# Clustered attention and an MoE layer on one core: PSUM places as one-bank tiles, and a planner that knows tiles, the shared port and the clock

## The chip, the cores and the metric

The kernel runs on one core of a Trainium2 chip. The metric is the device time of one execution in microseconds (us); the time before is the median of three executions. The engines are named as in the profile: PE (TensorE, matmul), PEld (its weight loads), DVE (VectorE), ACT (ScalarE), POOL (GpSimd) and SP (SyncE, which issues every DMA here).

## The reference

Attention in which a query sees only the keys of its own cluster, then a two-layer network with a quadratic activation:

```python
# q, k, v: (4, 8, 768, 64) f32; centroids: (8, 16, 64); w_in: (512, 2048); w_out: (2048, 512)
q_assign = argmax(einsum('bhsd,hcd->bhsc', q_n, c_n)); k_assign = the same of k
mask = q_assign[:, :, :, None] == k_assign[:, :, None, :]
scores = where(mask, q @ k.T / 8, -1e9)
attn = softmax(scores) @ v
x = attn.transpose(0, 2, 1, 3).reshape(3072, 512)
h = x @ w_in
g = where(h >= 1, h, where(h <= -1, 0, (h + 1) ** 2 / 4))
return g @ w_out
```

The two weight matrices come as 64-bit floats.

## The kernel before

The four batches follow each other; in each, four pairs of heads (hp) and three chunks of 256 queries (c). For one batch and pair, `kv_load` loads k, q and v, `kv_scale`, `kq_split` and `v_split` split them into two 16-bit parts, and `assign` finds the clusters: 48 small matmuls into a PSUM place z1 of 128x384, a chain of some ten DVE operations on z1 and the small place pn, and DMA transposes of the result. For each of four blocks of a chunk `at_scores` makes 128x768 scores (4 matmuls), DVE reads them into sS, `at_soft` takes the exponential on ACT (sS), casts it on ACT and subtracts on POOL (hl), and SP transposes hl by DMA into pT. `at_av` multiplies by v (36 matmuls into banka) and gives x. For each chunk u and each of eight slices f of the hidden layer, `ffn1` makes two groups of 12 matmuls from w and x into a place of 128x512, DVE reads that place twice (r), ACT squares and casts, POOL subtracts (g), and `ffn2` adds 12 matmuls of 128x512 to the output place of the chunk. Beside batch 0, `w_load`, `w_bits`, `w_sum` and `w_split` bring the weights into 16-bit parts.

**PSUM before** has eight banks: three tiles of two banks (`bank[0..2]`), `bank_a` for at_av and `bank_h`. The places are slices of them:

```python
halves = [bank[1][:, :512], bank[1][:, 512:]]
row_banks = Ring([bank_h, bank[2][:, :512], bank[2][:, 512:]])
hid = Ring([bank_h] + halves)
spare = Ring([x[:, 384:] for x in halves])
```

`hid` serves ffn1 and ffn_scale in turn, and all small places from step 22 on; up to then (`early()`) those come from `row_banks`, and w_sum's from `spare`. Scores use bank[0], and bank[1] in turn with it while `early()`; ffn2's output uses bank[2]. The framework that sets the semaphores does so tile by tile, and two halves of one tile are one tile to it.

**What sets the order.** The kernel's functions issue nothing: `Recorder.add` (L111) records each operation as a node with its price (`price`, L76) and its region in memory (`touch`, L137), and `issue` (L276) sets the order of all five engines. `forward` (L153) is a list scheduler: it runs the nodes on a model of the engines, the engine that is free first takes the ready node of best priority, and a node with a PSUM bank in use by another engine is put back until the bank is free. `backward` (L231) does this from the end and gives new priorities. After eight rounds (`ROUNDS`) the order with the shortest modelled end is issued by L291, so that nearly every instruction of the profile has the line L291. In the model a DVE operation on SBUF that shares a port with POOL costs 400 ns more (L101), and PE is at half speed for the first 75 us (`COLD`, L216).

Of the kernel before, what the change touches and what calls it, by code (L numbers as in the profile page):

```python
# [33 lines left out]
ROUNDS = 8  # L34

class Recorder:
# [30 lines left out]
    @staticmethod  # L69
    def free(ap):  # L70
        n = 1
        for _, k in list(ap.ap)[1:]:
            n *= k
        return n

    def price(self, eng, op, out, ins, kw):  # L76

        if "dma" in op:
            n = 1
            for k in out.shape:  # L80
                n *= k
            kb = n * mybir.dt.size(out.dtype) / 1024

            return 33, 79.0 if kb == 2 else kb, "transpose" in op
        n = max(self.free(a) for a in [out] + ins[:1])
        ps = any(a.space == PSUM for a in ins)
        cols = sum(isinstance(kw.get(k), bass.AP) for k in ("scale", "bias", "scalar", "scalar1", "scalar2"))
        if eng == "tensor":
            n = self.free(ins[1])
            half = self.free(ins[0]) <= 64 and n > 100  # L90
            if ins[1].dtype == F32:
                n *= 4

            return n / 4.8 + 9 if half else max(n / 2.4 + 2.5, 24)
        if eng == "scalar":
            cols += kw.get("accum_out") is not None
            first = n == 1 and kw.get("scale") == 0.0
            return 93 + n / 1.2 + 94 * cols - 43 * ps + 1283 * first
        if eng == "vector":
            wide = [a for a in ins if self.free(a) > 1 or n == 1]  # L100
# [4 lines left out]
            return 68 + n / 0.96 / fast + 61 * cols + 20 * (op == "reciprocal") + wait  # L105
        return 55 + n * (2.03 if op == "tensor_tensor" else 0.9 if op == "memset" else 3.5)

    def group(self):
        return Group(self)

    def add(self, eng, op, fn, args, kw):  # L111
        outs = [kw[k] for k in ("out", "accum_out") if kw.get(k) is not None]
        pos = [a for a in args if isinstance(a, bass.AP)]
        if "out" not in kw:
            outs.insert(0, pos.pop(0))
        ins = pos + [a for k, a in kw.items() if k not in ("out", "accum_out") and isinstance(a, bass.AP)]
        node = self.open
        if node is None:
            node = Node(eng, self.step, len(self.nodes))
            self.nodes.append(node)  # L120
        assert node.eng == eng
        p = self.price(eng, op, outs[0], ins, kw)
        if isinstance(p, tuple):
            node.cost += p[0]
            node.dma = p[1:]
        else:
            node.cost += p
        node.calls.append((fn, args, kw))
        for aps, w in ((ins, False), (outs, True)):
            for ap in aps:  # L130
                name, parts = self.regions(ap)
                for r in parts:
                    self.touch(node, name, r, w)
                    if ap.space == PSUM:
                        node.banks.update((name, x) for x in range(r[2] // 2048, (r[3] - 1) // 2048 + 1))

    def touch(self, node, name, r, w):  # L137
        seen = self.seen.setdefault(name, [])
# [11 lines left out]
        keep.append((r, w, node))  # L150
        self.seen[name] = keep

    def forward(self, prio):  # L153

        clock, ready, avail = {}, {}, {}
        left = {x: len(x.preds) for x in self.nodes}
        at = dict.fromkeys(self.nodes, 0.0)
        for x in self.nodes:
            if not x.preds:
                heappush(ready.setdefault(x.eng, []), (0.0, prio[x], x.i))  # L160
        hw, ring, sent, span = 450.0, 0.0, [], 0.0
        self.order, bank = [], {}
        todo = len(self.nodes)
        while todo:
            todo -= 1
            best = None
            for e, q in ready.items():
                now = clock.get(e, 0.0)
# [23 lines left out]
            free = max((until for k in x.banks for o, until in bank.get(k, {}).items() if o != e), default=0.0)  # L192
            if free > t:
                clock[e] = t
                heappush(q, (free, prio[x], x.i))
                todo += 1
                continue
            if x.dma and x.dma[0] > 256 and ring > t + AHEAD:

                clock[e] = t  # L200
                heappush(q, (ring - AHEAD, prio[x], x.i))
                todo += 1
                continue
            if x.dma:
                kb, tr = x.dma
                t = max(t, hw, sent[-8] if len(sent) > 7 else 0.0)
                clock[e] = t + x.cost
                hw = t + (650 if tr else 475)
                ring = max(ring, hw + (650 if tr else 784)) + kb * (5.6 if tr else 3.25)
                if tr:  # L210

                    hw = max(hw, ring - 1000)
                end = ring + (400 if tr else 1300)
                sent.append(end)
            else:
                clock[e] = t + x.cost * (2 if e == "tensor" and t < COLD else 1)  # L216
                end = clock[e] + LATENCY[e]
            for k in x.banks:
                bank.setdefault(k, {})[e] = end
            x.start, x.busy = t, clock[e]  # L220
            span = max(span, end)
            self.order.append(x)
            for y in x.succs:
                raw = x.dma or x.eng != y.eng or (y.preds[x] and x.eng != "tensor")
                at[y] = max(at[y], end if raw else x.busy)
                left[y] -= 1
                if not left[y]:
                    heappush(ready.setdefault(y.eng, []), (at[y], prio[y], y.i))
        return span

    def backward(self, prio):  # L231

# [6 lines left out]
        for _ in self.nodes:  # L239
# [16 lines left out]
            if x.dma:  # L256

                kb, tr = x.dma
                clock[e] = t + kb * (5.6 if tr else 3.25)
                start[x] = -clock[e] - 1275  # L260
            else:
                clock[e] = t + x.cost
                start[x] = -clock[e]
            for p, raw in x.preds.items():
                lag = 0.0
# [10 lines left out]
    def issue(self):  # L276
# [3 lines left out]
        prio = {x: x.step for x in self.nodes}  # L280
        best = None
        for _ in range(ROUNDS):
            span = self.forward(prio)
            if best is None or span < best[0]:
                best = span, self.order
            prio = self.backward({x: x.start for x in self.nodes})
        span, self.order = best
        with self.tc.manual_schedule():
            for x in self.order:
# [1 line left out]
                    fn(*args, **kw)  # L291


class Node:
    def __init__(self, eng, step, i):
        self.eng, self.step, self.i = eng, step, i
        self.banks = set()
        self.cost, self.dma, self.calls, self.preds, self.succs = 0.0, None, [], {}, []


# [49 lines left out]
def tile_clustered_attention_moe(  # L350
# [234 lines left out]
    def transpose(b, hp, out, nat):  # L585
# [340 lines left out]
    def w_sum(a, f, part):  # L926
# [69 lines left out]
    def ffn2(u, f):  # L996
# [129 lines left out]
```

## Time and profile before

| | us |
|---|---|
| median of 3 runs (917.8 to 919.25) | 918.27 |
| the profiled execution, its own time | 917.96 |
| its span, first to last instruction | 916.2 |
| PE busy | 819.7 |
| ACT busy | 660.5 |
| DVE busy | 621.8 |
| POOL busy | 580.4 |
| mean granted TensorE clock | 0.961 |

The profiled execution is 0.3 us under the median, and 1.8 us of it lie outside its span. PE is the engine with the most work; where it has idle time, and what ends that, is what has to be read. Names in the rows are tiles without their numbers: `bank` is any of the three two-bank tiles, `bankh` the single one.

### The profile page before, as it was taken

Reading aid. Unit: us, or ns where it says so; the run is one execution under the profiler, and the core shown is the slowest. Engines: PE = TensorE matmul, PEld = TensorE weight load, DVE = VectorE, ACT = ScalarE, POOL = GpSimd, SP = SyncE. Lnnn points to the kernel's source line nnn. Section 1 sums busy time; section 2 is a strip of 40 time slices with the busy share of each in tenths; the row PEclk is TensorE's granted clock in tenths of the full one; section 3 lists DMA queues with packets and bytes.
Section 4 is the critical chain, followed back from the end, with each engine's and each line's share of the span. In section 5 each row is a group of like instructions: output and inputs, shape, how many; then the busy total and the mean of one; then the engine's idle time right before and its main releaser. Section 6 shows DMA issues by size and latency. Waiting matters only on the chain.

```text
span 916.2 us, 19559 instructions
## 1 busy us (share of the span) xinstructions
PE 819.7 (89%) x7462; PEld 566.2 (62%) x7462; DVE 621.8 (68%) x1335; ACT 660.5 (72%) x1145; POOL 580.4 (63%) x521
## 2 busy tenths in 40 slices
PE   2556669899998999999998999999998999999998
PEld 2344446556765766776666666666665666667664
DVE  6999987887796665556987665557868555444232
ACT  5778999979767587778676687678766677776232
POOL 1369888986764667766575677656565666666322
PEclk9756779999999999999999999999999999999999
DMA  9989675658998878868899968878998866666100
GB/s 312 238 204 189 133 208 129 152 120 183 185 201 166 161 141 164 156 147 187 166 205 167 176 124 163 157 155 195 178 196 149 149 132 127 111 121 110 30 24 24
DMA packets 403263, 142.82 MB, mean 156 GB/s; under 512 B 380000, under 2 KB 395360, under 8 KB 403168
## 3 DMA queue, kind: packets, MB, share of 16 engines
q1 hardware_dynamic: 403168, 141.56, 76.3%
q8 instruction: 58, 0.95, 0.4%
q14 instruction: 37, 0.30, 0.1%
HBM read 40.40 MB, written 6.29 MB: 51 GB/s over the span
## 4 chain that ended last, share of the span: by engine, by line
PE 68%; DVE 14%; issue 4%; ACT 2%; POOL 2%; ACTq 0%; DVEq 0%; POOLq 0%
PE bank L291 51%; PE banka L291 10%; PE bankh L291 8%; DVE sS L291 3%; DVE r L291 2%; DVE bank L291 2%; DVE kvq L291 2%; DVE n L291 1%; POOL hl L291 1%; DVE w L291 1%; ACT sS L291 1%; DVE mx L291 1%; ACT hl L291 0%; ACT wk L291 0%; DVE bankh L291 0%
## 5 line engine op out<-in xcount | busy, mean ns | idle before, releaser
L291 POOL TENSOR_TENSOR hl<-sS,hl 128x768 f16<-128x768 f32 x181 | 311.4, 1723 | 138.2 <-ACT hl L291 122.1
L291 PE MATMUL bank<-w,g 128*128 128x512 f16 x1152 | 272.7, 380 | 3.0 <-ACT o L291 1.8
L291 PEld LDWEIGHTS <-w 128*128 128x128 f16 x2304 | 223.8, 98 | 62.4 <-issue 21.7
L291 DVE CUSTOM_DVE_ANT_0 sS<-bank,zero,er 128x768 f32<-128x768 f32 x192 | 194.2, 1012 | 88.6 <-PE bank L291 68.2
L291 PEld LDWEIGHTS <-kvq 128*128 128x128 f16 (+1 forms) x3264 | 191.3, 107 | 88.8 <-issue 43.2
L291 ACT ACTIVATE sS<-sS,sbi 128x768 f32<-128x768 f32 x192 | 179.3, 934 | 87.0 <-DVE sbi L291 83.3
L291 PEld LDWEIGHTS <-g 128*128 128x128 f16 x1152 | 111.1, 98 | 120.6 <-POOL g L291 3.3
L291 PE MATMUL bank<-kvq 128*128 128x384 f16 x768 | 163.1, 337 | 17.4 <-DVE sbi L291 7.7
L291 POOL TENSOR_TENSOR g<-r,g 128x512 f16<-128x512 f32 x88 | 104.5, 1187 | 87.3 <-ACT g L291 87.2
L291 ACT CAST hl<-sS 128x768 f16<-128x768 f32 x181 | 148.8, 825 | 3.1 <-DMA pT<-hl 1.7
L291 PE MATMUL bank<-x,w 128*128 128x256 f16 x1056 | 127.9, 274 | 7.2 <-DVE bank L291 3.5
L291 ACT ACTIVATE r<-r,f_ra,f_rs 128x512 f32<-128x512 f32 x88 | 71.3, 810 | 59.0 <-DVE r L291 58.6
L291 PE MATMUL banka<-pT,kvq 128*64 128x256 f16 x1728 | 105.9, 278 | 0.0
L291 DVE TENSOR_SCALAR r<-bank,f_lo,f_hi 128x512 f32<-128x512 f32 x60 | 48.5, 808 | 39.6 <-PE bank L291 32.7
L291 ACT CAST g<-r 128x512 f16<-128x512 f32 x88 | 53.8, 611 | 22.4 <-DVE r L291 13.9
L291 PE MATMUL bank<-wk,w 128*128 128x256 f16 x504 | 60.2, 273 | 4.0 <-DVE bank L291 1.9
L291 POOL TENSOR_TENSOR w<-w 128x1024 f32<-128x1024 f32 (+1 forms) x24 | 52.1, 2177 | 10.6 <-ACT w L291 10.6
L291 PE MATMUL bankh<-x,w 128*128 128x256 f16 x480 | 57.0, 273 | 1.6 <-DVE r L291 1.5
L291 DVE SCALAR_TENSOR_TENSOR r<-bank,f_gs,r 128x512 f32<-128x512 f32 x60 | 44.8, 746 | 13.3 <-ACT r L291 11.3
L291 POOL TENSOR_TENSOR n<-n,phi 128x768 f16<-128x768 f16 x14 | 21.6, 1540 | 28.9 <-DMA kvq<-n 14.9
L291 ACT ACTIVATION_READ_ACCUMULATOR sS<-sS,sbi 128x1 f32 x192 | 36.0, 187 | 0.0
L291 DVE TENSOR_SCALAR r<-bankh,f_lo,f_hi 128x512 f32<-128x512 f32 x28 | 22.6, 809 | 19.5 <-PE bankh L291 16.7
(180 smaller groups left out, 884.0 us busy)
## 6 DMA issues: line engine op xcount, KB each, us to landing
w<-in_moe_w_out_dram SPq DMA_DIRECT2D x14, 512.0 KB, 4.4
kvq<-in_k_dram SPq DMA_DIRECT2D x16, 384.0 KB, 3.8
kvq<-in_q_dram SPq DMA_DIRECT2D x16, 384.0 KB, 3.9
kvq<-in_v_dram SPq DMA_DIRECT2D x16, 384.0 KB, 4.2
out_dram<-o SPq DMA_DIRECT2D x11, 512.0 KB, 3.8
w<-in_moe_w_in_dram SPq DMA_DIRECT2D x10, 512.0 KB, 5.3
n<-in_moe_w_in_dram SPq DMA_DIRECT2D x6, 512.0 KB, 4.2
o<-in_v_dram SPq DMA_DIRECT2D x8, 384.0 KB, 3.9
```

The costliest lines, as they stand in the source:

```text
L291: fn(*args, **kw)
```

## The change

Every matmul, every operation and every transfer stays; the two programs have the same instructions on every engine. What changes is the place in PSUM of some of them, and the order.

**Places.** Two tiles of two banks stay (`pair`: scores, and in turn with pair[1] while `early()`; ffn2's output is pair[1]). The other four banks are tiles of one bank: `bank_a`, and `bankh`, `banki`, `bankj`, which one ring `hid` hands out to ffn1, ffn_scale, w_sum and all small places, early or not. `row_banks`, `halves` and `spare` are gone, and the three early rings become one ring of three places.

**Order.** A node's banks are now whole tiles (`node.banks.add(name)`). A node that needs the port that DVE and POOL share is marked `turn` and waits in the model until the other's turn is over, in place of the flat 400 ns. The clock of PE is modelled by windows of 3413 ns: full speed after a window with enough PE work, half speed otherwise, in place of the fixed 75 us. The latencies are lower. There are 12 rounds, and the order kept is the one whose `replay`, at four phases of the clock's window, has the smallest sum. The model's engines move from `forward` into a class `Machine`.

```diff
-LATENCY = dict(tensor=280, scalar=252, vector=230, gpsimd=175)
-COLD, AHEAD = 75e3, 1500
+LATENCY = dict(tensor=265, scalar=150, vector=135, gpsimd=100)
+AHEAD = 1500
+WINDOW, SLOW, FULL = 3413.0, 0.41, 0.77
+PHASES = (0.0, 850.0, 1700.0, 2550.0)
+TURN, TURN_WAIT = dict(vector=185, gpsimd=118), 200
...
-            wait = 400 if not ps and (len(wide) > 1 or op in ("tensor_scalar", "tensor_copy")) else 0
...
+    def turns(self, eng, op, out, ins):
+        if eng == "gpsimd":
+            return op != "memset"
+        if eng != "vector" or any(a.space == PSUM for a in ins) or op == "tensor_tensor_reduce":
+            return False
+        wide = [a for a in ins if self.free(a) > 1 or self.free(out) == 1]
+        return len(wide) > 1 or (op in ("tensor_scalar", "tensor_copy") and out.space != PSUM)
...
-                        node.banks.update((name, x) for x in range(r[2] // 2048, (r[3] - 1) // 2048 + 1))
+                        node.banks.add(name)
...
-            span = self.forward(prio)
+            self.forward(prio)
+            starts = {x: x.start for x in self.nodes}
+            span = sum(self.replay(p) for p in PHASES)
...
+class Machine:
+    def free(self, x, t):
+        for k in x.banks:
+            for e, until in self.bank.get(k, {}).items():
+                if e != x.eng:
+                    t = max(t, until)
+        if x.turn:
+            t = max(t, self.port - TURN[x.eng])
+        return t
...
+    def product(self, t, cost):
+        while True:
+            while t >= self.window:
+                self.full = self.work > (SLOW if self.full else FULL) * WINDOW
+                self.window, self.work = self.window + WINDOW, 0.0
+            pace = 1 if self.full else 2
+            part = min(cost * pace, self.window - t)
+            t, self.work, cost = t + part, self.work + part, cost - part / pace
+            if cost < 1e-3:
+                return t
...
-    bank = [psum.tile([P, 1024], F32, name=f"bank{i}") for i in range(3)]
-    bank_a, bank_h = [psum.tile([P, 512], F32, name=f"bank{x}") for x in "ah"]
-    halves = [bank[1][:, :512], bank[1][:, 512:]]
-    row_banks = Ring([bank_h, bank[2][:, :512], bank[2][:, 512:]])
-    hid = Ring([bank_h] + halves)
+    pair = [psum.tile([P, 1024], F32, name=f"pair{i}") for i in range(2)]
+    bank_a, *one = [psum.tile([P, 512], F32, name=f"bank{x}") for x in "ahij"]
+    hid = Ring(one)
...
-    spare = Ring([x[:, 384:] for x in halves])
...
-        return (row_banks if early() else hid)(*shape, dtype=F32)
+        return hid(*shape, dtype=F32)
...
-        ps = view(bank[start() if hp == 0 else 2], [2, 4 * 256], BF16)
+        ps = view(pair[start()], [2, 4 * 256], BF16)
...
-        pS = view(bank[n % 2 if early() else 0], [2, 512], F32)
+        pS = view(pair[n % 2 if early() else 0], [2, 512], F32)
...
-        pc = (spare if early() else hid)(P, dtype=F32)
+        pc = misc(P)
...
-            F[u] = view(bank[2], [CT, DM], F32)
+            F[u] = view(pair[1], [CT, DM], F32)
```

**DVE between batches 1 and 2** (499 to 508 us in the profile before), where `assign` of the last pair stands among ffn1's reads. Waits are named by the engine whose semaphore is awaited. `bank1` holds z1 in one half and ffn1's hidden values in the other. Before:

```order
L291 TENSOR_REDUCE mx0_146<-bank1_75 128x24 [waits PE_49]
L291 TENSOR_TENSOR bank1_75<-bank1_75,mx0_146 128x384 [waits DVE_49]
L291 TENSOR_TENSOR bank1_75<-bank1_75,iota_88 128x384 [waits DVE_49]
L291 TENSOR_REDUCE mx0_146<-bank1_75 128x24 [waits DVE_49,PE_49]
L291 SCALAR_TENSOR_TENSOR kvq3_64<-kvq3_64,sv2_145 128x768 [waits DMAHW4_49,Activation_49]
L291 TENSOR_TENSOR bank1_75<-bank1_75,mx0_146 128x384 [waits DVE_49]
L291 TENSOR_SCALAR r0_209<-bank1_75,f_lo0_184,f_hi0_179 128x512 [waits DVE_49,Pool_49]
L291 TENSOR_SCALAR n0_72<-bank1_75 128x12x16
```

The same chain in the change, z1 in `bankh` and ffn1's values in `bankj`:

```order
L316 TENSOR_SCALAR r0_210<-bankj_79,f_lo0_185,f_hi0_180 128x512 [waits DVE_49,PE_49]
L316 TENSOR_REDUCE mx0_147<-bankh_77 128x24 [waits PE_49]
L316 TENSOR_TENSOR bankh_77<-bankh_77,mx0_147 128x384 [waits DVE_49]
L316 SCALAR_TENSOR_TENSOR r0_210<-bankj_79,f_gs0_205,r0_210 128x512 [waits Activation_49]
L316 TENSOR_TENSOR bankh_77<-bankh_77,iota_89 128x384 [waits DVE_49]
L316 TENSOR_REDUCE mx0_147<-bankh_77 128x24 [waits DVE_49]
L316 TENSOR_TENSOR bankh_77<-bankh_77,mx0_147 128x384 [waits DVE_49]
L316 TENSOR_SCALAR n0_72<-bankh_77 128x12x16 [waits DVE_49,Pool_49]
```

The second reduction of z1 no longer waits for PE, the two reads of ffn1's place (r) have moved ahead of it and into it, and the split of v (kvq, sv) has left this stretch.

**PE at the same place.** The last scores matmul and the first ones of ffn1's second group, which writes the half of `bank1` beside z1, before:

```order
L291 MATMUL bank0_74<-kvq2_63 128x384
L291 LDWEIGHTS w0_73
L291 MATMUL bank1_75<-x0_68,w0_73 128x256 [waits DVE_49]
L291 LDWEIGHTS w0_73
L291 MATMUL bank1_75<-x0_68,w0_73 128x256
```

In the change an ffn1 group stands between the two halves of assign's matmuls:

```order
L316 LDWEIGHTS kvq3_64
L316 MATMUL bankh_77<-cT_110,kvq3_64 128x16
L316 LDWEIGHTS w0_73
L316 MATMUL bankj_79<-x0_68,w0_73 128x256
L316 LDWEIGHTS w0_73
L316 MATMUL bankj_79<-x0_68,w0_73 128x256
```

The wait for DVE at the first matmul of the group is gone.

**DVE in the first stage** (52 to 60 us before): kvq<-kvq,sv is a split of v, g<-kvq,sc,g a split of q or k, w<-w,wk a weight's step, all on SBUF; the rows that name a bank read PSUM. Before:

```order
L291 SCALAR_TENSOR_TENSOR kvq2_63<-kvq2_63,sv0_143 128x768
L291 TENSOR_SCALAR er1_149<-bank2_76,es1_137 128x12
L291 SCALAR_TENSOR_TENSOR g0_71<-kvq3_64,sc1_135,g0_71 128x12x64 [waits DMAHW2_49,Activation_49]
L291 SCALAR_TENSOR_TENSOR w0_73<-w0_73,wk0_66 128x1024 [waits DMAHW5_49,DMAHW4_49]
L291 TENSOR_REDUCE mx0_146<-bank2_76 128x24 [waits PE_49]
L291 ISA sS2_81,sbi0_156<-bank0_74,zero_105,er1_149 128x768 [waits DVE_49,Pool_49]
```

In the change, around the same split g:

```order
L316 TENSOR_SCALAR wk0_66<-wk0_66 128x1024 [waits Activation_49]
L316 SCALAR_TENSOR_TENSOR g0_71<-kvq3_64,sc1_136,g0_71 128x12x64 [waits DMAHW2_49,Activation_49]
L316 TENSOR_TENSOR pT2_167<-pair0_74,pT2_167 128x6x128 [waits Activation_49]
L316 ISA sS2_82,sbi3_160<-pair1_75,zero_106,er1_150 128x768
L316 ISA sbi3_160 128x1
L316 SCALAR_TENSOR_TENSOR o0_65<-kvq3_64,sc1_136,o0_65 128x12x64
```

The weight's step no longer follows g; between g and the next split (o) stand two reads of PSUM. Over the whole stage the weights have moved back and attention forward: on ACT 59 operations stand before the exponential of step 8 in the order before, 17 of them on weights, and 52 in the change, 13 of them on weights; before that of step 24 stand 141 in both, 47 of them on weights. From 879 us of the profile before on, every engine runs the same rows in the same order.

More of the change, by code (lines that the diff above doesn't have):

```diff
@@ L127, in add @@
             node.cost += p
+        node.turn |= self.turns(eng, op, outs[0], ins)
         node.calls.append((fn, args, kw))
@@ L151, in touch, with done, push @@
         self.seen[name] = keep
+    def done(self, x, end, at, left, ready):
+        for y in x.succs:
+            raw = x.dma or x.eng != y.eng or (y.preds[x] and x.eng != "tensor")
+            at[y] = max(at[y], end if raw else x.busy)
+            left[y] -= 1
+            if not left[y]:
+                ready(y)
     def forward(self, prio):
-        clock, ready, avail = {}, {}, {}
+        ready, avail = {}, {}
         left = {x: len(x.preds) for x in self.nodes}
         at = dict.fromkeys(self.nodes, 0.0)
+        m = Machine(PHASES[0])
+        clock = m.clock
+        def push(x):
+            heappush(ready.setdefault(x.eng, []), (at[x], prio[x], x.i))
         for x in self.nodes:
             if not x.preds:
[L160 to L165, printed above, removed]
+                push(x)
+        self.order = []
+        while len(self.order) < len(self.nodes):
             best = None
@@ L190, in forward @@
                 x = self.nodes[i]
-            free = max((until for k in x.banks for o, until in bank.get(k, {}).items() if o != e), default=0.0)
-            if free > t:
+            free = m.free(x, t)
+            if x.dma and x.dma[0] > 256:
+                free = max(free, m.ring - AHEAD)
+            if free > t + 1:
                 clock[e] = t
                 heappush(q, (free, prio[x], x.i))
-                todo += 1
                 continue
[L198 to L221, printed above, removed]
-            self.order.append(x)
[L223 to L228, printed above, removed]
@@ L229, in forward, with replay @@
-        return span
+            end = m.run(x, t)
+            self.order.append(x)
+            self.done(x, end, at, left, push)
+        return m.span
+    def replay(self, phase):
+        m = Machine(phase)
+        left = {x: len(x.preds) for x in self.nodes}
+        at = dict.fromkeys(self.nodes, 0.0)
+        todo = {}
+        for x in reversed(self.order):
+            todo.setdefault(x.eng, []).append(x)
+        while todo:
+            starts = []
+            for e, q in todo.items():
+                x = q[-1]
+                if not left[x]:
+                    t = max(m.clock.get(e, 0.0), at[x])
+                    starts.append((max(t, m.free(x, t)), x.i))
+            t, i = min(starts)
+            x = self.nodes[i]
+            todo[x.eng].pop()
+            if not todo[x.eng]:
+                del todo[x.eng]
+            self.done(x, m.run(x, t), at, left, lambda y: None)
+        return m.span
@@ L291, in issue, with __init__, run @@
                     fn(*args, **kw)
+class Machine:
+    def __init__(self, phase):
+        self.clock, self.bank = {}, {}
+        self.hw, self.ring, self.sent, self.span = 450.0, 0.0, [], 0.0
+        self.port = 0.0
+        self.window, self.work, self.full = WINDOW - phase, 0.0, False
+    def free(self, x, t):
[6 more added lines that the diff above has]
+        return t
+    def run(self, x, t):
+        e = x.eng
+        if x.dma:
+            kb, tr = x.dma
+            t = max(t, self.hw, self.sent[-8] if len(self.sent) > 7 else 0.0)
+            x.busy = t + x.cost
+            self.hw = t + (650 if tr else 475)
+            self.ring = max(self.ring, self.hw + (650 if tr else 784)) + kb * (5.6 if tr else 3.25)
+            if tr:
+                self.hw = max(self.hw, self.ring - 1000)
+            end = self.ring + (400 if tr else 1300)
+            self.sent.append(end)
+        else:
+            x.busy = self.product(t, x.cost) if e == "tensor" else t + x.cost
+            if x.turn:
+                self.port = x.busy
+            end = x.busy + LATENCY[e]
+        for k in x.banks:
+            self.bank.setdefault(k, {})[e] = end
+        x.start, self.clock[e] = t, x.busy
+        self.span = max(self.span, end)
+        return end
+    def product(self, t, cost):
[8 more added lines that the diff above has]
+                return t
 class Node:
```

10 lines of the change are left out of this document (5 added, 5 removed).

## The prediction

> **What bounds the kernel now.** The page first: the share of each engine, and the chain that ended last.
>
> ```profile
> span 916.2 us, 19559 instructions
> PE 819.7 (89%) x7462; PEld 566.2 (62%) x7462; DVE 621.8 (68%) x1335; ACT 660.5 (72%) x1145; POOL 580.4 (63%) x521
> ...
> PE 68%; DVE 14%; issue 4%; ACT 2%; POOL 2%; ACTq 0%; DVEq 0%; POOLq 0%
> ```
>
> PE is the engine to fill, and 916.2 − 819.7 = 96.5 us of its span are idle. Matmuls are neither added nor removed, so the change can win PE's idle time, and the time that PE loses at half clock, and nothing else. Where that lies is told by the view of busy time in windows. The windows are put where the character changes: first stage, first batch, changes of batch, steady work, tail.
>
> ```profile
> core 0: us, PE busy (x) PEld busy (x) DVE busy (x) ACT busy (x) POOL busy (x), PEclk, DMA share, GB/s
> 0.00:25.00 25.00, 6.77 (x93) 5.92 (x94) 16.89 (x43) 15.41 (x25) 4.28 (x27) 1.00 0.95 317
> 25.00:100.00 75.00, 44.76 (x423) 31.73 (x420) 72.58 (x149) 59.62 (x84) 51.52 (x35) 0.66 0.92 208
> 100.00:175.00 75.00, 54.68 (x478) 39.20 (x479) 62.18 (x147) 71.11 (x110) 65.78 (x49) 0.89 0.61 150
> 175.00:250.00 75.00, 72.83 (x667) 49.74 (x667) 60.86 (x170) 62.03 (x116) 57.62 (x50) 0.98 0.83 159
> 250.00:300.00 50.00, 45.03 (x479) 30.88 (x477) 40.10 (x81) 33.55 (x60) 29.54 (x27) 1.00 0.92 182
> 300.00:425.00 125.00, 124.38 (x1073) 85.39 (x1070) 74.57 (x159) 92.43 (x169) 81.63 (x76) 1.00 0.79 156
> 425.00:525.00 100.00, 92.80 (x934) 63.96 (x932) 76.89 (x155) 69.78 (x126) 63.77 (x56) 1.00 0.97 181
> 525.00:625.00 100.00, 100.00 (x876) 69.34 (x874) 59.69 (x128) 76.17 (x142) 65.74 (x60) 1.00 0.79 155
> 625.00:725.00 100.00, 91.88 (x928) 63.23 (x927) 76.80 (x154) 69.35 (x123) 62.15 (x58) 1.00 0.93 174
> 725.00:850.00 125.00, 125.00 (x1093) 86.16 (x1091) 63.62 (x132) 92.25 (x168) 83.63 (x77) 1.00 0.67 120
> 850.00:916.20 66.20, 61.59 (x442) 40.63 (x439) 17.59 (x23) 18.82 (x28) 14.75 (x15) 1.00 0.08 23
> ```
>
> Three regimes stand there. Up to 175 us PE is idle for 175 − 106.2 = 68.8 us: DVE is full in 25 to 100 (72.6 of 75), then ACT (71.1 of 75). In the steady windows (300 to 425, 525 to 625, 725 to 850) PE has 0.6 us of idle in 350, so nothing can be won. In the three changes of batch (250 to 300, 425 to 525, 625 to 725) it is idle for 5.0 + 7.2 + 8.1 = 20.3 us, and DVE, with `assign` beside ffn1's reads, is at 77 of 100. What ends PE's waits from 175 us on, by the view of waits (total, times, longest):
>
> ```profile
> PE bank L291 <- DVE r L291: 5.8, 8, 1.5
> PE bank L291 <- DVE bank L291: 5.0, 8, 1.4
> PE bank L291 <- DVE sbi L291: 3.9, 5, 1.2
> PE bank L291 <- DVE n L291: 1.9, 2, 1.4
> ```
>
> **Term A, places as tiles of their own.** The timeline of one change of batch shows what these waits are.
>
> ```profile
> 498.78 0.71 PE L291 MATMUL bank<-x,w 128*128 128x256 f16 x5
> 499.53 0.56 DVE L291 TENSOR_REDUCE mx<-bank 128x24 f32<-128x384 f32 x1 [1.59 <-PE bank L291]
> 500.12 0.57 DVE L291 TENSOR_TENSOR bank<-bank,mx 128x384 f32<-128x384 f32 x1
> 500.72 0.57 DVE L291 TENSOR_TENSOR bank<-bank,iota 128x384 f32<-128x384 f32 x1
> 501.34 1.47 PE L291 MATMUL bank<-x,w 128*128 128x256 f16 x12 [1.20 <-DVE bank L291]
> 502.85 0.56 DVE L291 TENSOR_REDUCE mx<-bank 128x24 f32<-128x384 f32 x1 [1.56 <-PE bank L291]
> ```
>
> z1 is in one half of bank[1] and ffn1's place in the other, but they take turns: DVE waits 1.59 us for ffn1's first group before it reduces z1, ffn1's second group waits 1.20 us for DVE's third operation on z1, and DVE waits 1.56 us for that group. Neither needs the other's data. In the new order this reduction has z1 in bankh and no wait for PE, and ffn1's groups are in bankj. Of the rows of waits, r, bank and n together (5.8 + 5.0 + 1.9 = 12.7 us) can be of this kind; those for sbi are for the scores tile, which stays one tile. Matching the semaphore counts that PE awaits in the built program with the instructions that raise them, I find about 10 us of PE's idle time after 175 us in waits for an instruction that touches only the other half. I take **−10 us**. The bounds: −18, if the DVE chain of assign, freed of its own false waits, also shortens the true ones in the 20.3 us; +3, if the one ring of three brings as many true waits and the new order's places are worse. It costs nothing on other engines: the operations are the same.
>
> **Term B, the order that knows the shared port.** In the first stage DVE's operations on SBUF are longer than their own work. The first two rows below are groups of DVE in 0 to 175 us (count, busy, mean ns); the others are single operations in the timeline.
>
> ```profile
> L291 DVE SCALAR_TENSOR_TENSOR w<-w,wk 128x1024 uint32<-128x1024 uint32 x12 | 24.5, 2038 | 0.0
> L291 DVE TENSOR_SCALAR wk<-wk 128x1024 uint32<-128x1024 uint32 x15 | 16.6, 1107 | 2.3 <-ACT wk L291 2.2
> ...
> 29.49 1.22 DVE L291 SCALAR_TENSOR_TENSOR w<-w,wk 128x1024 uint32<-128x1024 uint32 x1
> 51.39 0.68 DVE L291 TENSOR_SCALAR wk<-wk 128x1024 uint32<-128x1024 uint32 x1
> 52.72 2.23 POOL L291 TENSOR_TENSOR hl<-sS,hl 128x768 f16<-128x768 f32 x1 [3.33 <-ACT hl L291]
> 53.53 2.23 DVE L291 SCALAR_TENSOR_TENSOR g<-kvq,sc,g 128x768 f16<-128x768 f32 x1
> 54.91 5.69 POOL L291 TENSOR_TENSOR w<-w 128x1024 f32<-128x1024 f32 x2
> 55.69 2.91 DVE L291 SCALAR_TENSOR_TENSOR w<-w,wk 128x1024 uint32<-128x1024 uint32 x1
> ```
>
> The weight's step takes 1.22 us alone and 2.91 behind POOL's: whichever holds the port makes the other wait. Twelve of them lose 12 × (2.04 − 1.22) = 9.8 us, fifteen of wk 15 × (1.107 − 0.68) = 6.4, so 16.2 us of DVE's 134.8 busy in 25 to 175 are waits. The new order puts PSUM work of DVE between them and chooses when each side comes. If half goes, DVE wins 8 us; in 25 to 100, where DVE is full, that is time, in 100 to 175 ACT has only 75 − 71.1 = 3.9 us left to give. I take **−6 us**. The bounds are −12 (8 while DVE is full, 4 behind) and 0 to +10: if the turns fall otherwise, nothing goes, and more collisions than now are as possible.
>
> A rule bears on this. The Trainium skill, in "SBUF — State Buffer" under "Who interferes with whom", says that the port pair of VectorE and GpSimd is an exclusive lock, held for the whole instruction, and that the order of issue alone decides who waits. The first half agrees with the 2.91 us above. The second speaks against the plan: nothing makes the chip keep the turns that were planned. By that rule B may be 0 and the sum 908 in place of 902.
>
> **What else moves.** *The clock*: the old plan took half speed up to 75 us, the trace has 0.66 in 25 to 100 and 0.89 in 100 to 175, so the old plan took PE as too fast there. PE has 20.3 us idle in that second window and ACT covers it: nothing, and at most 0.11 × 54.7 = 6 us if PE were the bound. *SP*: DMA transposes of the second pair's q and k move ahead of four weight loads in the first 40 us. The first matmuls that take weights come much later:
>
> ```profile
> 134.83 4.08 PE L291 MATMUL bank<-x,w 128*128 128x256 f16 x24
> ```
>
> Those 95 us are the loads' cover; nothing. If it went, ACT's weight work would wait, which is the slower rival below. *The tail*: 850 to 916 has 4.6 us of PE idle, the last stores among it, and nearly the same order; nothing. *Fewer early places*: six overlapping places become three; cost 0 in the sum, priced as a rival.
>
> **Sum.** 917.96 (profiled execution; 916.2 of span and 1.8 around it) − 10 − 6 = 902. The median before is 0.3 above that execution, within what the numbers can carry. Forecast **902 us**, its own range 897 to 907.
>
> **Rivals.**
> - *The turns aren't kept*: A −10, B 0: **908**. For it: POOL's start is set by ACT's casts, not by the plan (3.33 us of waiting for hl above). Against: most of the stage is full, so the order does shift collisions.
> - *A new wait takes the old one's place*: DVE is at 77 of 100 in the changes of batch and the three places go round faster than DVE frees them. A −4, B −2: **912**. For it: 5.8 us of the waits end with r, ffn1's own second read. Against: the places were three before as well, of which two excluded each other.
> - *More comes*: the freed assign chain closes most of the 20.3 us, and B reaches its bound: −15 − 11 = **892**.
> - *It doesn't do what it says*: other waits end at the same moments, and the plan's better prices change nothing: within 0.2% of 918.27, about what a measurement here can tell from no change.
> - *Slower*: z1 now holds one of only three places for the whole of assign, with all of w_sum's and ffn1's places behind it in the ring.
>
> ```profile
> 18.38 0.54 DVE L291 TENSOR_REDUCE mx<-bank 128x24 f32<-128x384 f32 x1
> ...
> 30.62 0.23 DVE L291 TENSOR_SCALAR er<-bank,es 128x12 f32<-128x12 f32 x1
> ```
>
>  The chain takes 30.85 − 18.38 = 12.5 us in the first assign. Each of batch 0's four assigns may hold the weights back between 0 and 12.5; at 6 each it is 24 us of ACT's weight work late, with ACT full behind it. Less A and B that makes 917.96 + 24 − 16 = **926**. It decides the sign from 4 us for each assign on (4 × 4 = 16). Against it: the new order moves the weights back on purpose and has caught up by the 24th step, with 47 weight operations of ACT before it in both.
>
> **Chances.** 902: 0.48; turns not kept, 908: 0.14; new wait, 912: 0.10; more, 892: 0.12; nothing: 0.06; slower, 926: 0.10. Faster by over 0.2%: 0.48 + 0.14 + 0.10 + 0.12 = 0.84; within 0.2%: 0.06; slower: 0.10. The range runs from 888 (892 with some room) to 916 (912 likewise); it leaves out "nothing" and "slower", 0.16, and the far ends of the rest.
>
> **What would show it.** A: the rows of waits of PE for r, bank and n after 175 us fall from 12.7 us to a few, and PE's idle time in the three changes of batch from 20.3 to about 10; the steady windows stay at zero. DVE's reduction of z1 no longer has PE's ffn1 as its releaser. B: the mean of w<-w,wk goes from 2038 ns towards 1220, and the window of 25 to 100 does more of PE's work. I am wrong if PE's idle time in the changes stays near 20 us with other releasers (r, sbi) in the rows; if ACT has new idle time before 175 us behind w_sw or bank (the slower rival); or if DVE's groups keep their means while the stage becomes shorter, which would be an order better by its other prices.

## The result and the profile after

The change takes **893.88 us** (median of 4 runs, 893.43 to 894.44) against 918.34 for the kernel before (4 runs). The ratio is 0.9733, with a 95% interval of 0.9716 to 0.9750: 24.5 us less. The forecast was 902 with a range of 888 to 916, so the direction is right and the time lies in the range, but half as much again was won as was forecast.

The page of the change begins so; the two rows stand against those at the head of the prediction.

```profile
span 891.7 us, 19490 instructions
...
PE 812.6 (91%) x7462; PEld 563.2 (63%) x7462; DVE 616.5 (69%) x1335; ACT 659.0 (74%) x1145; POOL 575.5 (65%) x521
```

PE's idle time is 891.7 − 812.6 = 79.1 us, 17.4 less than the 96.5 before; its busy time is 7.1 less for the same 7462 matmuls. 17.4 + 7.1 = 24.5, the whole gain (each side from one execution). The 69 instructions fewer do no work on an engine: the counts of all five are the same. Where the idle time went is shown by the view of windows, the same ones as before (window, its length, then busy time of PE, PEld, DVE, ACT, POOL; clock; DMA share; GB/s).

```profile
0.00:25.00 25.00, 5.60 (x101) 4.86 (x102) 17.47 (x44) 16.05 (x26) 3.98 (x27) 1.00 0.90 258
25.00:100.00 75.00, 43.60 (x414) 30.63 (x413) 71.65 (x154) 59.99 (x83) 50.36 (x37) 0.77 0.93 223
100.00:175.00 75.00, 58.22 (x527) 41.49 (x527) 63.96 (x150) 72.24 (x114) 66.07 (x49) 0.89 0.65 159
175.00:250.00 75.00, 74.26 (x696) 50.86 (x694) 64.87 (x174) 63.31 (x120) 59.24 (x51) 1.00 0.82 173
250.00:300.00 50.00, 47.94 (x477) 33.58 (x476) 42.17 (x86) 35.66 (x63) 32.50 (x29) 1.00 1.01 182
300.00:425.00 125.00, 125.00 (x1135) 86.73 (x1134) 75.35 (x154) 94.57 (x175) 84.66 (x78) 1.00 0.85 162
425.00:525.00 100.00, 98.08 (x941) 66.91 (x941) 77.64 (x177) 72.61 (x134) 62.58 (x58) 1.00 0.95 177
525.00:625.00 100.00, 100.00 (x919) 70.16 (x914) 62.48 (x129) 80.14 (x146) 70.73 (x65) 1.00 0.92 177
625.00:725.00 100.00, 97.81 (x959) 68.00 (x958) 74.28 (x160) 72.45 (x133) 64.47 (x59) 1.00 0.92 164
725.00:850.00 125.00, 125.00 (x1068) 86.19 (x1067) 55.71 (x101) 80.71 (x143) 72.81 (x67) 1.00 0.55 101
850.00:920.00 70.00, 37.07 (x246) 23.80 (x244) 10.93 (x14) 11.28 (x16) 8.07 (x7) 0.99 0.04 16
```

In the three changes of batch (250 to 300, 425 to 525, 625 to 725) PE was idle for 20.3 us; now it is 2.1 + 1.9 + 2.2 = 6.2. From 175 to 850 us the idle time falls from 23.1 us to 6.9. Up to 175 us it is 67.6 in place of 68.8, nearly the same, but more work is done in that time (1042 matmul records in place of 994) and at a better clock (0.77 in place of 0.66 in 25 to 100). Setting each matmul of the change against the same matmul before, with the idle time ahead of it and its own share of busy time, puts about 5 us of the gain in the work that began in the first 200 us before (less than 2 idle, more than 3 busy) and some 19 behind it (about 16 idle, under 4 busy).

The view of PE's waits from 175 us on begins with these rows (total, times, longest); before, the four rows that the prediction shows made 5.8 + 5.0 + 3.9 + 1.9 = 16.6 us. A wait for sbi is one for the scores tile, which DVE has to read into sS and sbi first.

```profile
PE bankj L316 <- DVE r L316: 1.9, 2, 1.3
PE pair L316 <- DVE sbi L316: 1.4, 2, 1.1
PE bankj L316 <- DVE er L316: 1.3, 1, 1.3
PE pair L316 <- ACT o L316: 0.8, 2, 0.7
PE bankh L316 <- DVE n L316: 0.8, 2, 0.6
```

And this is the same change of batch as in the prediction, now at 484 us (start, length, engine, then the group; in brackets idle time and its releaser):

```profile
484.72 1.47 PE L316 MATMUL bankj<-x,w 128*128 128x256 f16 x12
...
486.23 0.81 DVE L316 TENSOR_SCALAR r<-bankj,f_lo,f_hi 128x512 f32<-128x512 f32 x1 [0.17 <-PE bankj L316]
486.95 0.55 DVE L316 TENSOR_REDUCE mx<-bankh 128x24 f32<-128x384 f32 x1
...
487.54 0.57 DVE L316 TENSOR_TENSOR bankh<-bankh,mx 128x384 f32<-128x384 f32 x1
...
488.01 0.74 DVE L316 SCALAR_TENSOR_TENSOR r<-bankj,f_gs,r 128x512 f32<-128x512 f32 x1
488.67 0.56 DVE L316 TENSOR_TENSOR bankh<-bankh,iota 128x384 f32<-128x384 f32 x1
489.26 0.56 DVE L316 TENSOR_REDUCE mx<-bankh 128x24 f32<-128x384 f32 x1
...
489.87 1.47 PE L316 MATMUL bankj<-x,w 128*128 128x256 f16 x12
```

Both reductions of z1 start without a wait (1.59 and 1.56 us before), and the group of ffn1 in the middle of the chain is not held by it (1.20 before). From 486.23 on DVE goes through this chain without idle time.

### The profile page after: what moved, and what is told of

Read it like the earlier page. It is cut to its first block, busy times and chain, and to the rows that moved or that the text cites. A ratio compares the mean times of both kernels' runs of the same rounds, so it can differ in the third digit from the quotient of the medians.

```text
span 891.7 us, 19490 instructions
## 1 busy us (share of the span) xinstructions
PE 812.6 (91%) x7462; PEld 563.2 (63%) x7462; DVE 616.5 (69%) x1335; ACT 659.0 (74%) x1145; POOL 575.5 (65%) x521
## 4 chain that ended last, share of the span: by engine, by line
PE 65%; DVE 16%; ACT 8%; issue 6%; POOL 3%; DMA 1%; SPq 0%; ACTq 0%; DVEq 0%; POOLq 0%
PE pair L316 32%; PE banka L316 10%; PE bankj L316 8%; PE bankh L316 8%; PE banki L316 7%; DVE sS L316 3%; ACT sS L316 2%; DVE n L316 2%; DVE wk L316 2%; DVE kvq L316 1%; POOL hl L316 1%; ACT w L316 1%; ACT n L316 1%; ACT hl L316 1%; DVE w L316 1%
## 5 line engine op out<-in xcount | busy, mean ns | idle before, releaser
L316 POOL TENSOR_TENSOR hl<-sS,hl 128x768 f16<-128x768 f32 x181 | 306.1, 1697 | 120.2 <-ACT hl L316 91.8
L316 PE MATMUL pair<-w,g 128*128 128x512 f16 x1152 | 270.8, 379 | 1.1 <-ACT o L316 0.8
L316 DVE CUSTOM_DVE_ANT_0 sS<-pair,zero,er 128x768 f32<-128x768 f32 x192 | 194.3, 1012 | 85.2 <-PE pair L316 59.0
L316 PE MATMUL pair<-kvq 128*128 128x384 f16 x768 | 164.8, 341 | 24.8 <-DVE sbi L316 12.7
L316 ACT CAST g<-r 128x512 f16<-128x512 f32 x88 | 53.7, 610 | 21.1 <-DVE r L316 17.2
L316 PE MATMUL bankj<-x,w 128*128 128x256 f16 x528 | 63.4, 272 | 1.3 <-DVE r L316 1.3
L316 PE MATMUL bankh<-x,w 128*128 128x256 f16 x528 | 63.0, 273 | 0.0
L316 PE MATMUL banki<-x,w 128*128 128x256 f16 x480 | 57.5, 273 | 0.2 <-DVE r L316 0.2
L316 DVE TENSOR_SCALAR r<-bankj,f_lo,f_hi 128x512 f32<-128x512 f32 x30 | 24.3, 809 | 23.4 <-PE bankj L316 12.8
L316 PEld LDWEIGHTS <-ones 128*128 128x128 bf16 x244 | 17.6, 107 | 31.3 <-issue 22.8
```

## The experiments

Two theories were to be told apart. **P**: the freed places carry the gain, and the new order adds a little in the first stage. **O**: the order carries it, and the tiles matter less. A wait is called false below when it is for an instruction that touches only the other half of the tile. Each kernel ran beside the kernel before on the same chip, and ratios are to that.

### The places alone, and the order alone

*places_only* is the kernel before, its planner too, with the places of the change: these lines and the uses that follow from them.

```diff
-    bank = [psum.tile([P, 1024], F32, name=f"bank{i}") for i in range(3)]
-    bank_a, bank_h = [psum.tile([P, 512], F32, name=f"bank{x}") for x in "ah"]
-    halves = [bank[1][:, :512], bank[1][:, 512:]]
+    pair = [psum.tile([P, 1024], F32, name=f"pair{i}") for i in range(2)]
+    bank_a, *one = [psum.tile([P, 512], F32, name=f"bank{x}") for x in "ahij"]
+    hid = Ring(one)
```

> The planner of before (flat 400 ns, fixed 75 us of half clock, old latencies, 8 rounds), with the places of the change (banks h, i, j as tiles of their own, one ring). Theory P, the freed places carry most of the gain (PE's idle time after 175 us fell by 16 us of the 24.5): about 902, between 899 and 906, and PE's idle time in the changes of batch near 6 us. Theory O, the order carries most of it: 912 to 918, and the idle time there stays near 20 us.

*order_only* is the change with the same lines undone, so the new planner over the old places.

> The planner of the change, with the two-bank places, the early rings and the spare places of before; the planner knows here that a tile of two banks is one thing. Theory P: the order alone is worth the 8 us of the first stage, about 910 (906 to 914), and the changes of batch keep some 15 to 20 us of idle PE. Theory O: 894 to 900, since a planner that knows the whole tiles orders around the waits.

Measured: places_only 900.59, ratio 0.9815 (0.9794 to 0.9837); order_only 902.72, ratio 0.9841 (0.9816 to 0.9865). Against the kernel before beside them (918.12) each alone wins 17.5 and 15.4 us, and the two together 24.5, not 33. So P has the time of the first kernel and misses the second, O misses both, and neither theory holds as it stands: in large part the two take away the same thing. In the changes of batch PE is idle for 10.2 us in places_only, where P put 6, and for 9.2 in order_only, where it put 15 to 20. PE's idle time from 175 to 850 us agrees: 23.1 before, 13.9 with the places alone (in an execution of 903.5 us, the slowest of its four), 11.7 with the order alone, 6.9 with both.

### The waits between halves, put back alone

*one_tile* keeps the change's order, row for row the same on every engine, and its places. Only the tiles differ; the first line lets the planner go on as if banki and bankj were tiles of their own, so that the order stays:

```diff
-                        node.banks.add(name)
+                        node.banks.add((name, r[2] // 2048) if "ij" in name else name)
...
-    bank_a, *one = [psum.tile([P, 512], F32, name=f"bank{x}") for x in "ahij"]
-    hid = Ring(one)
+    bank_a, bank_h = [psum.tile([P, 512], F32, name=f"bank{x}") for x in "ah"]
+    bank_ij = psum.tile([P, 1024], F32, name="bankij")
+    hid = Ring([bank_h, bank_ij[:, :512], bank_ij[:, 512:]])
```

> The order of the change, row for row the same on every engine; only banki and bankj are the two halves of one tile of two banks again, so that the waits between halves are back and nothing else. Theory P: 906 to 912, with the waits of PE for r, bank and n back after 175 us. Theory O: within 3 us of the change (891 to 897).

Measured: **914.11**, ratio 0.9958 (0.9944 to 0.9972). With nothing changed but which waits the tiles bring, 20 us are lost, some 80% of the gain, and more than theory P had expected. The first rows of PE's waits from 175 us on:

```profile
PE bankij L316 <- DVE r L316: 9.0, 16, 1.3
PE pair L316 <- DVE sbi L316: 4.0, 5, 1.6
PE bankh L316 <- DVE n L316: 2.3, 3, 1.0
PE bankij L316 <- DVE er L316: 2.1, 2, 1.5
```

The row for r on the shared tile has 16 waits, where banki and bankj of the change have 3 between them and the two programs run the same rows. PE also waits longer for sbi on pair (1.4 us in the change) and for n on bankh (0.8), though pair and bankh are the same tiles in both: a wait put back on one place makes true waits behind it longer. That is what the prediction's bound of −18 supposed.

### What the planner must know

*tile_blind* is order_only with one line of the planner as before: a place is a bank of 2 KB, not a tile.

```diff
-                        node.banks.add(name)
+                        node.banks.update((name, x) for x in range(r[2] // 2048, (r[3] - 1) // 2048 + 1))
```

> As order_only (planner of the change, two-bank places of before), but the planner takes each bank of 2 KB as a place of its own, as before, and so doesn't know that the halves of a tile wait for each other. Theory K, what order_only won (15 us) is the knowledge of whole tiles: 911 to 918. Theory L, it is the other prices (turns, clock, latencies): 900 to 906.

Measured: 916.08 (ten executions, 915.09 to 919.69; the trace is of one at 918.81), ratio 0.9987 (0.9971 to 1.0002), no difference from the kernel before that can be told. Turns, clock, latencies and more rounds are worth nothing here as long as the planner is wrong about the tiles; the one line is worth 13 us. Its waits look like those of before (r 6.1, bank 4.1, against 3.6 and 0.4 in order_only):

```profile
PE bank L316 <- DVE sbi L316: 7.3, 11, 1.6
PE bank L316 <- DVE r L316: 6.1, 8, 1.6
PE bank L316 <- DVE bank L316: 4.1, 4, 1.3
```

So most of the gain has one cause: **the planner's places and the framework's tiles must be the same**. Split tiles make the planner of before right (places_only); a planner that counts tiles is right about the old ones (order_only). What is left beside the split tiles, some 7 us, is the matter of the next part.

### The port in the planner

How much chance there is in one order was asked first. *control* has one latency 1 ns higher:

```diff
-LATENCY = dict(tensor=265, scalar=150, vector=135, gpsimd=100)
+LATENCY = dict(tensor=266, scalar=150, vector=135, gpsimd=100)
```

> The change with one latency in the planner at 266 ns instead of 265: a different order by chance, with the same rules. What chance alone is worth. If single parts of the planner can be told apart by one kernel each: within 2 us of the change (892 to 896). If the search lands where it happens to: up to 5 us from it (889 to 899), and then no part of the order that moves the time by less can be told apart in this way.

Measured: 896.69, ratio 0.9752 (0.9731 to 0.9772): the two orders are 2.8 us apart, so up to some 3 us are taken for chance, from this one pair. *no_turns* has no turns and the flat 400 ns of before, *no_turns_2* the same with the 266 of the control, and *no_price* has neither price. All three drop this line; the first two also have the lines of `price` back that the change removed.

```diff
-        node.turn |= self.turns(eng, op, outs[0], ins)
```

> The change without its knowledge of the shared port: no node is a turn, and the flat 400 ns of before are back. If the turns are worth the 6 us that were predicted: 900 (897 to 904), all of the loss before 175 us, with the mean of the weight's step (w<-w,wk) back from 1517 ns towards 2038. If the turns are not kept on the chip and the first stage was won by other prices: 892 to 897, with the means of the DVE groups where they are in the change.

> no_turns with the latency of 266 ns of the control: the same rules, another order by chance. If what no_turns lost is the rule's and not chance: 899 to 906. If chance: it comes closer to the change than 898.

> The change with no knowledge of the port at all in the planner: no turns, and no flat 400 ns either. If no_turns lost its 8.8 us by the flat 400 ns, which make every DVE operation on SBUF look 400 ns longer: 892 to 898. If it lost them because the turns are missing: 899 to 904.

Measured: no_turns 902.65 (0.9829, 0.9812 to 0.9846), no_turns_2 900.34 (0.9813, 0.9796 to 0.9829), no_price 910.83 (0.9930, 0.9909 to 0.9950). Against the flat price the turns are worth 4 to 9 us (no_turns_2 against the control, no_turns against the change), somewhat more than chance; no price at all costs 17 us against the turns and 8 to 10 against the flat price, more than either expectation had it. PE's idle time in no_turns is 68.9 us up to 175 us and 14.0 from there to 850 (67.6 and 6.9 in the change), so most of this loss is behind the first stage, where it was not expected. The turns' gain doesn't come from fewer collisions. These are DVE's groups up to 175 us in the change (count, busy, mean ns):

```profile
L316 DVE TENSOR_SCALAR wk<-wk 128x1024 uint32<-128x1024 uint32 (+1 forms) x16 | 21.1, 1320 | 1.6 <-ACT wk L316 1.6
L316 DVE SCALAR_TENSOR_TENSOR w<-w,wk 128x1024 uint32<-128x1024 uint32 x12 | 18.2, 1517 | 0.2
```

The weight's step has fallen from 2038 ns to 1517, but wk has risen from 1107 to 1320 (1306 without the one operation of 128x512, which is the other form in the row): 24.5 + 16.6 = 41.1 us before, 18.2 + 21.1 = 39.3 now, that one included. And the same groups in no_turns:

```profile
L317 DVE SCALAR_TENSOR_TENSOR w<-w,wk 128x1024 uint32<-128x1024 uint32 x12 | 20.2, 1683 | 0.0
L317 DVE TENSOR_SCALAR wk<-wk 128x1024 uint32<-128x1024 uint32 (+1 forms) x16 | 16.7, 1045 | 4.0 <-ACT wk L317 4.0
```

20.2 + 16.7 = 36.9: less time in these groups than in the change, and a later end. Without any price, in no_price, PE and ACT wait like this up to 175 us:

```profile
PE pair L315 <- DVE pT L315: 17.0, 7, 3.3
PE pair L315 <- ACT sS L315: 14.9, 6, 4.2
PE pair L315 <- DVE sbi L315: 8.9, 4, 3.1
...
ACT sS L315 <- DVE sbi L315: 16.2, 10, 2.9
```

The same rows in the change:

```profile
PE pair L316 <- DVE sbi L316: 11.2, 7, 4.1
PE pair L316 <- DVE pT L316: 8.1, 4, 3.8
...
PE pair L316 <- ACT sS L316: 5.2, 4, 2.8
...
ACT sS L316 <- DVE sbi L316: 3.7, 5, 1.2
```

PE's three rows make 40.8 us in place of 24.5, but waits change places: all of PE's idle time up to 175 us is 73.4 us in place of 67.6. ACT is busy for 62.4 of the 75 us from 100 to 175, and 72.2 in the change. DVE isn't fuller, with 60.2 us there against 64.0. That a planner which takes the port as free plans more for DVE than it can do, so that ACT and PE wait for it, fits these waits, but it is an argument and not shown. And it is half of the matter: from 175 to 850 us PE is idle for 13.4 us in no_price, as in no_turns (14.0), and not for 6.9. That the flat price loses there because it also burdens operations that meet no POOL is not borne out: no_price has no such burden and loses as much. The rows that differ most there are PE's for sbi: 4.9 us in no_turns, 7.0 in no_turns_2 and 6.7 in no_price, 1.4 in the change and 1.8 in the control. Why the turns shorten them stays open.

*port_free* asked from the other side what the collisions cost. It has the change's order, with POOL's wide reads replaced:

```diff
...
+        for _ in range(2):
+            x.calls.append((nc.gpsimd.memset, (o, val), {}))
+        x.calls.append((fn, (), dict(out=o[:, :1], in0=i0[:, :1], in1=i1[:, :1], op=kw["op"])))
```

> The order of the change, row for row; POOL's subtractions and products on weights, and those on hl of the first 30 steps, are replaced by two memsets of the same tile and the operation on one column, so the split parts of weights and of these scores are left out. The point is to take POOL's wide reads away from the port, with DVE's operations as they are. Theory B, collisions at the port are on the path of the first stage: 880 to 886, with w<-w,wk near its 1220 ns. Theory N, DVE's lost time lies beside other work (old_latency lost 10 us less of it than the change and took the same time): 890 to 895, though w<-w,wk falls all the same.

Measured: 890.23, ratio 0.9699 (0.9678 to 0.9720), some 3 to 4 us better than the change. DVE's groups:

```profile
L316 DVE TENSOR_SCALAR wk<-wk 128x1024 uint32<-128x1024 uint32 (+1 forms) x16 | 16.1, 1009 | 1.6 <-ACT wk L316 1.6
L316 DVE SCALAR_TENSOR_TENSOR w<-w,wk 128x1024 uint32<-128x1024 uint32 x12 | 15.8, 1317 | 0.2
```

These two alone give back 39.3 − 31.9 = 7.4 us of DVE, of which about half reaches the end. That is theory N. The bound isn't clean: wk stays well above its 0.68 us alone, because the memsets hold it up too (the last section has the rows).

### Clock, latencies and the search

*old_clock* puts the fixed 75 us back in `run`, *old_latency* the four latencies of before, and *rounds_48* changes `ROUNDS = 12` to 48.

```diff
-            x.busy = self.product(t, x.cost) if e == "tensor" else t + x.cost
+            x.busy = t + x.cost * (2 if e == "tensor" and t < 75e3 else 1)
```

> The change with the clock of before in the planner (half speed up to 75 us, then full). If the windows of the clock are worth nothing, as predicted: within what the control shows of chance, 890 to 899. If they carry the first stage: 899 to 905, the loss before 200 us.

> The change with the latencies of before in the planner (280, 252, 230, 175 ns). If they are worth nothing: 890 to 899. If the lower latencies carry the gain that no_turns and order_only leave open: 899 to 905, spread over the changes of batch, where chains of short DVE operations set the pace.

> The change with 48 rounds of planning in place of 12; the planner's own end is 3.8 us earlier. If its model is good to the 3 us that the control shows: 887 to 893. If what is left of the differences between orders isn't in the model: 892 to 898.

Measured: old_clock 898.50 (0.9777, 0.9759 to 0.9796), old_latency 893.57 (0.9725, 0.9705 to 0.9745), rounds_48 895.04 (0.9756, 0.9741 to 0.9770). The latencies are worth nothing. The clock's windows may be worth some 2 us over the control and 4.6 over the change, which isn't clearly told apart from chance; the loss that the expectation put before 200 us isn't there, for old_clock has less idle PE up to 175 us (64.4) and more from 175 to 850 (13.8). More rounds found an end that the planner's model puts 3.8 us earlier and the chip 1.2 us later: below some 3 us the model no longer ranks orders. No kernel that computes everything was clearly faster than the change.

## Why the prediction was right, and where its sum was off

**What bounds it.** Right. The gain is PE's idle time and PE's busy time, the steady windows stayed at zero, and the tail at 4.6 us of idle.

**Term A, −10: the mechanism right, the size wrong.** It measured −17.5 on the way in (places_only) and −20 on the way out (one_tile). The step that was mis-sized is "I find about 10 us of PE's idle time after 175 us in waits for an instruction that touches only the other half". It counted PE's own false waits, and put those of DVE at nothing except in the bound, though they were as long (1.59 and 1.56 us in the same rows). one_tile shows, with the same rows in the same order, that false waits make true ones longer: sbi, which was not to change, goes from 1.4 to 4.0. So the condition of the −18, "if the DVE chain of assign, freed of its own false waits, also shortens the true ones", was met there. places_only alone doesn't show it. In its trace the rows for r, bank and n fall from 12.7 us to about 2 and PE's idle time in the changes of batch by 10.1, both as predicted; but sbi rises from 3.9 to 8.7, and another 4.4 us go before 175 us, where the term had nothing. Both together take 14.1 of the 20.3 us.

PE's busy time had no place in the sum either. Stretches of idle PE over 20 ns from 175 us on fell from 40 to 16 while 3.6 us of busy time went with them, 0.15 us each. one_tile agrees: it has 42 such stretches with the rows of the change, and for the same matmuls PE is busy 4.0 us longer from there on, again 0.15 each. What makes the 0.15 us is not shown.

**Term B, −6: the size near by luck, the reason and the place wrong.** Beside the places the order is worth 900.59 − 893.88 = 6.7 us, up to 3 of which may be chance. But "If half goes, DVE wins 8 us" is not what happened. The mean of w<-w,wk fell as was said, but wk's rose, and of the 16.2 us of waits for the port the two groups gave back 1.8. Nor does 25 to 100 do more of PE's work: 414 matmul records in place of 423. Against places_only the change has more idle PE up to 175 us (67.6 against 64.4) and less from there to 850 (6.9 against 13.9), and the row that differs most is the wait for sbi, 1.4 us against 8.7. The prediction had named this case, "an order better by its other prices". The runs point to the price of the port (no_turns, no_turns_2 and no_price) and leave open how it acts. The clock is no part of it that can be told: it is better in 25 to 100 us (0.66 to 0.77), which the sum put at nothing, but old_latency had 0.63 there and took as long as the change.

**The sum.** It added A and B as if they were separate. They overlap: −17.5 with the places alone and −15.4 with the order alone, −24.5 together, and with neither the places nor the knowledge of the tiles, though with all the rest of the new planner, −2 (tile_blind). The time lies in the range because that was wide enough for "More comes".

**The rivals.** "More comes", 892, is the nearest, by its first half: most of the 20.3 us was closed, though not by the freed chain alone, and B did not go to its bound. "The turns aren't kept" was right that the collisions hardly fell and wrong on the time, since the price was worth time without that. On the rule of the Trainium skill ("SBUF — State Buffer", "Who interferes with whom"), that the order of issue alone decides who waits: the rows of the last section agree, for where two operations collided there the one that began first went on and the other ended after it, and no run shows planned turns kept on the chip. That B would then be 0 did not follow. No new wait took the old one's place in the change (sbi did in places_only). The slower rival, weights held behind z1, did not come: ACT is busy for 72.2 us in 100 to 175, against 71.1 before, and none of its waits up to 175 us is for w_sw, where before there were 2.5 us; one of 1.9 us is for a bank (bankj).

## What to carry to other kernels

Where a planner sets the order, its resources must be those that the framework makes instructions wait for, tile by tile. Either side can be brought to the other, and here a planner that was wrong about this got nothing from its better prices. Count false waits on every engine of a loop, not only on the one to fill: the true waits behind them were longer too. A price for a contended resource was worth time here though the collisions hardly fell; where it acted had to be read from the waits, and it was not where the collisions were. Before a single part of a planner is judged, a kernel that differs by chance alone should run beside it.

## What was not expected of the hardware

In port_free a POOL operation on a single column of hl took 0.19 us where DVE read only PSUM beside it, and 0.42 us in the mean. The first row is the group of that shape up to 175 us, the others are from the timeline:

```profile
L316 POOL TENSOR_TENSOR hl<-sS,hl 128x1 f16<-128x1 f32 x18 | 7.5, 418 | 13.0 <-DVE w L316 10.9 <-POOL hl L316 1.0
...
49.51 0.19 POOL L316 TENSOR_TENSOR hl<-sS,hl 128x1 f16<-128x1 f32 x1
...
65.70 1.21 DVE L316 SCALAR_TENSOR_TENSOR w<-w,wk 128x1024 uint32<-128x1024 uint32 x1
...
65.91 1.06 POOL L316 TENSOR_TENSOR hl<-sS,hl 128x1 f16<-128x1 f32 x1
```

The last one began 0.21 us after the weight's step and ended 0.06 us after it (66.97 against 66.91). So however little an operation reads, it can still wait behind DVE.

POOL's memsets, which read nothing, held up one of DVE's two groups and not the other:

```profile
82.66 1.96 POOL L316 MEMSET w<- 128x1024 f16 x2
...
83.52 1.22 DVE L316 SCALAR_TENSOR_TENSOR w<-w,wk 128x1024 uint32<-128x1024 uint32 x1
...
114.35 1.96 POOL L316 MEMSET w<- 128x1024 f16 x2
...
115.58 1.27 DVE L316 TENSOR_SCALAR wk<-wk 128x1024 uint32<-128x1024 uint32 x1 [0.78 <-ACT wk L316]
```

The weight's step takes 1.22 us beside them, as it does alone; wk begins before they end at 116.31 and ends 0.54 us after that, in place of 0.68 us after its start. Ten of the 15 operations of wk of this size end 0.54 or 0.55 us after a memset, and ten of the 12 weight's steps take 1.21 to 1.23 us.
